# Start of a two-branch token mixer: copies behind their own transposes, 1/std spread ahead of the third group, C of block 1 held, one more warm-up matmul

## Chip, cores, metric

One core of one Trainium2 chip. The metric is the device time of one execution in microseconds (us). The profile's span is about 1.75 us shorter than the time of the same execution; differences of spans and of times can be compared with each other. Batches of runs were on different chips, so each run is compared with runs of the kernel before that were made beside it on its own chip, unless something else is said.

## The reference, cut to what matters

```python
xn = layernorm(x)                       # x: 2048 tokens x 576, bf16
# branch A: a diagonal complex state space model, 576 states, scanned over the tokens
h[t] = Lam_bar * h[t-1] + B_bar @ xn[t]
y[t] = 2 * Re(C @ h[t]) + xn[t] * Dskip
# branch B: a gated unit, 576 -> 4608 -> 576
b = (sigmoid(xn @ w_gate) * (xn @ w_up)) @ w_down
out = x + y + b
```

The kernel works on four blocks of 512 tokens. The gated unit's products (gate/up groups and `w_down` pairs) fill TensorE. The scan runs on VectorE beside them, and "C of block nb" is the product of C with the states of one block, added to the output of that block.

## The kernel before: the parts concerned

The first ten groups of block 0 are "raw": they multiply centred but not yet scaled x, and the scale 1/std per token is put in when a group is emptied from PSUM. PSUM is four buffers of two banks (`ps`), and they are handed from user to user. The start:

```python
start_groups = [RawGateUp(0, f, 0) for f in range(2)]
ptrs = [psum.tile([P, 2, TB], FP32, name="ptr", tag="ps") for _ in range(2)]
def ptr(tt):                                   # tiles 0, 1 in buffer 0; tiles 2, 3 in buffer 1
    return ptrs[tt // 2][:, tt % 2, 0:6 * H].bitcast(BF16).rearrange(...)
...
busy(7, TB)                                    # warm-up: 7 matmuls of 512 columns on zeros
start_mean(0, nc.vector); start_mean(1, nc.scalar)
xc0 = start_centre(0, nc.vector); xc1 = start_centre(1, nc.scalar)
start_transpose(2, xts[2]); start_transpose(0, xc0)
start_transpose(1, xc1);    start_transpose(3, xts[3])
for tt in range(2):
    nc.vector.tensor_copy(xc_part(tt), ptr(tt)[:, 0:RC + 1, :])
start_mean(2, nc.scalar); start_mean(3, nc.scalar)
over_rows(pmean(2), negm[:, 2:3])              # spread a column over rows: an fp32 transpose
busy(4, P)
start_centre_rows(2)
for g in start_groups: g.turn(0, first)        # tokens 0 to 255
over_rows(pmean(3), negm[:, 3:4]); start_centre_rows(3)
for g in start_groups: g.turn(1, first)
... # squares, 1/std on ScalarE and VectorE, statistics of block 1 on VectorE
... # second halves of both groups (tokens 256 to 511)
third = RawGateUp(0, 2, 0); third.open(); third.turn(0)
consts_transpose(ptr(3)[:, RC, :])
for tt in range(TT_B):
    over_rows(ptrs[1][:, 0, tt * P:(tt + 1) * P], rstds[0][:, tt:tt + 1])
consts_copy(ptr(3)[:, RC, :])                  # three small copies on VectorE
nc.scalar.copy(scale0[:], ptrs[1][:, 0, :])    # the fourth group takes this buffer
```

And C of block 1, which is issued as soon as the last state operation of the block is queued:

```python
def between_steps():
    if 1 in ssm_done and 1 not in c_done and glu_done[0]:
        for tl in range(0, TT_B, 2):
            d_pair([TT_B + tl, TT_B + tl + 1], [c_terms(1, tl), c_terms(1, tl + 1)], True, True)
        c_done.add(1)
```

Of the kernel before, what the change touches and what calls it, by code (L numbers as in the profile page):

```python
# [12 lines left out]
FP32 = mybir.dt.float32  # L13
BF16 = mybir.dt.bfloat16
# [52 lines left out]
def kernel(  # L67
# [17 lines left out]
    nc = tc.nc  # L85
    P = 128
    H = 64
# [7 lines left out]
    TB = 512  # L95
# [3 lines left out]
    TT_B = TB // P  # L99
    KF = D // P  # L100
    R0 = KF * P
    PT = NS // P
    NU = PT + 1
# [3 lines left out]
    NH = D // H  # L107
    FP = 2
    RC = R0 // P
# [12 lines left out]
    hpool = ctx.enter_context(tc.tile_pool(name="hpool", bufs=1))  # L122
# [84 lines left out]
    cvals = consts.tile([P, 3, NU], FP32, name="cvals")  # L207
    ldt, lre, lim = (cvals[:, i, :] for i in range(3))
    def consts_transpose(ps):
        for half in (slice(0, H), slice(H, P)):  # L210
            nc.tensor.transpose(ps[half, 0:3 * NH], crows[:], ident[0:3 * NH, 0:3 * NH])

    def consts_copy(ps):

        rows = ps[:, 0:3 * NH].rearrange("p (i a) -> p i a", a=NH)
        nc.vector.tensor_copy(cvals[0:H, :, :], rows[0:H, :, 0:NH:2])
        nc.vector.tensor_copy(cvals[H:P, :, 0:PT], rows[H:P, :, 1:NH:2])
        nc.vector.tensor_copy(cvals[H:P, :, PT:NU], rows[H:P, :, NH - 1:NH])

    iota = ssmp.tile([P, TB], FP32, name="iota", tag="buim", bufs=2)  # L220
    nc.gpsimd.iota(iota[:], pattern=[[1, TB]], base=0, channel_multiplier=0,
# [8 lines left out]
    rstds = {}  # L230
# [5 lines left out]
    def ln_stats(tt):  # L236
        nb, tl = divmod(tt, TT_B)
        if tl == 0:
            mvs[nb] = lnp.tile([P, TT_B, nc.vector.BN_AGGR_DIM], FP32, name="mv")
            rstds[nb] = lnp.tile([P, TT_B], FP32, name="rstd")  # L240
        xt = xts[tt]
        st = lnp.tile([P, 2, BN], FP32, name="bnst")
        for gi in range(2):
            nc.vector.bn_stats(st[:, gi, :], xt[:, gi * DH:(gi + 1) * DH])
        nc.vector.bn_aggr(mvs[nb][:, tl, :], st[:])
# [8 lines left out]
    negm = consts.tile([P, TT_B], FP32, name="negm")  # L254
    ssq = consts.tile([P, TT_B], FP32, name="ssq")

    def start_mean(tt, eng):
        junk, m = xn_bufs[tt % 2], negm[:, tt:tt + 1]
        if eng is nc.vector:
            nc.vector.tensor_scalar(junk[:, 0:D], xts[tt][:], -1.0 / D, None, ALU.mult, ALU.add, accum_out=m)  # L260
        else:
            nc.scalar.activation(junk[:, 0:D], xts[tt][:], ACT.Copy, scale=-1.0 / D, accum_out=m)
# [188 lines left out]
    hst = {}  # L451
# [7 lines left out]
    def ssm_w(nb, pt, part):  # L459
        bre, bim = bu[(nb, pt)]  # L460
        t1, t2 = T1[:, pt, :], T2[:, pt, :]
        if part == 0:
            tmps["w"] = ssmp.tile([P, 2, TB], BF16, name="wrim", tag="wrim")
        w = tmps["w"][:, part, :]
        a, b = (bre, bim) if part == 0 else (bim, bre)
        tq = bft("tq", 2)
        nc.vector.tensor_mul(w, t1, a[:])
        nc.vector.tensor_mul(tq[:], t2, b[:])
        if part == 0 and pt < PT:
            nc.vector.tensor_sub(w, w, tq[:])  # L470
        else:
            nc.vector.tensor_add(w, w, tq[:])
# [32 lines left out]
    def ssm_h(nb, pt, part):  # L505
        gre, gim = tmps["gre"], tmps["gim"]
        c, s = C2[:, pt, :], S2[:, pt, :]
        tq = bft("tq", 2)
        if part == 0:
            h = hpool.tile([P, 2, TB], BF16, name="hst", tag="hst", bufs=10)  # L510
            hst[(nb, pt)] = h
            nc.vector.tensor_mul(h[:, 0, :], c, gre[:])
            nc.vector.tensor_mul(tq[:], s, gim[:])  # L513
            nc.vector.tensor_add(h[:, 0, :], h[:, 0, :], tq[:])  # L514
        else:
            h = hst[(nb, pt)]
            nc.vector.tensor_mul(h[:, 1, :], s, gre[:])
            nc.vector.tensor_mul(tq[:], c, gim[:])
            nc.vector.tensor_sub(h[:, 1, :], h[:, 1, :], tq[:])


    bg = Background()
# [130 lines left out]
    def c_terms(nb, tl):  # L653
        ts_ = slice(tl * P, (tl + 1) * P)
        terms = []
        for pt in range(PT):
            terms.append((hst[(nb, pt)][:, 0, ts_], ctre[:, pt, :]))
            terms.append((hst[(nb, pt)][:, 1, ts_], ctim[:, pt, :]))
        terms.append((hst[(nb, PT)][:, 0, ts_], ctp[:]))
        return terms  # L660
# [105 lines left out]
    glu_done = [False]  # L766
    ln_done = set()
    ssm_done = set()
    c_done = set()
    bu_wanted = deque()  # L770
    chain = [(nb, pt) for nb in range(NB) for pt in range(NU)]

    def want_bu(i):
        if i < len(chain):
            bu_wanted.append(chain[i])

    def queue_ssm(i):
        nb, pt = chain[i]

        def bu_ready():  # L780
            return (nb, pt) in bu and bu_at[(nb, pt)] + 2 <= bg.now

        def h_ready():
            return nb < 2 or (nb - 2) in c_done

        bg.add(1.85, lambda: ssm_w(nb, pt, 0), ready=bu_ready)
        if pt < PT:
            bg.add(1.85, lambda: ssm_w(nb, pt, 1))
        else:
            bg.add(0.0, lambda: None)  # L790
        bg.add(0.0, lambda: want_bu(i + 2))
        bg.add(1.3, lambda: ssm_scan(nb, pt, 0))
        bg.add(2.0 if pt < PT else 1.2, lambda: ssm_scan(nb, pt, 1))
        bg.add(1.3, lambda: ssm_h(nb, pt, 0), ready=h_ready)
        if pt < PT:
            bg.add(1.3, lambda: ssm_h(nb, pt, 1))
        if pt == NU - 1:
            bg.add(0.0, lambda: ssm_done.add(nb))


    n_slots = NSB * NC
# [36 lines left out]

    def between_steps():

        if 1 in ssm_done and 1 not in c_done and glu_done[0]:
            for tl in range(0, TT_B, 2):
                d_pair([TT_B + tl, TT_B + tl + 1], [c_terms(1, tl), c_terms(1, tl + 1)], True, True)
            c_done.add(1)
# [26 lines left out]
    start_groups = [RawGateUp(0, f, 0) for f in range(2)]  # L871
    ptrs = [psum.tile([P, 2, TB], FP32, name="ptr", tag="ps") for _ in range(2)]

    def ptr(tt):
        return ptrs[tt // 2][:, tt % 2, 0:6 * H].bitcast(BF16).rearrange("p (c t) -> p c t", t=P)

    def pmean(tt):
        return ptrs[tt // 2][:, tt % 2, 6 * H:8 * H]

    for g in start_groups:  # L880
        g.open()
# [1 line left out]
    def busy(n, cols):  # L883
        for i in range(n):
            zeros = warm[:].unsqueeze(1).to_broadcast([P, cols // P, P])
            nc.tensor.matmul(start_groups[0].ps[:, i % 2, 0:cols], warm[:], zeros, start=True, stop=True)

    def start_transpose(tt, src):
        for c in range(RC):
            nc.tensor.transpose(ptr(tt)[:, c, :], src[:, c * P:(c + 1) * P], ident[:])  # L890
        for rows in (LO, HI):
            nc.tensor.transpose(ptr(tt)[rows, RC, :], src[:, R0:D], ident[:])

    def over_rows(dst, col):
        nc.tensor.transpose(dst, col.to_broadcast([P, P]), ident32[:])  # L895

    def xc_part(tt):
        return xcT[:, :, tt * P:(tt + 1) * P]

    def start_centre(tt, eng):  # L900
        xc = xn_bufs[2 + tt]
        if eng is nc.vector:
            nc.vector.tensor_scalar_add(xc[:, 0:D], xts[tt][:], negm[:, tt:tt + 1])
        else:
            nc.scalar.activation(xc[:, 0:D], xts[tt][:], ACT.Identity, bias=negm[:, tt:tt + 1])
        return xc
# [5 lines left out]
        nc.vector.tensor_add(xc_part(tt), ptr(tt)[:, 0:RC + 1, :],  # L912
                             mrow[:, tt % 2, :].unsqueeze(1).to_broadcast([P, RC + 1, P]))

    busy(7, TB)
    start_mean(0, nc.vector)
    start_mean(1, nc.scalar)
    xc0 = start_centre(0, nc.vector)
    xc1 = start_centre(1, nc.scalar)
    start_transpose(2, xts[2])  # L920
    start_transpose(0, xc0)
    start_transpose(1, xc1)
    start_transpose(3, xts[3])
    for tt in range(2):
        nc.vector.tensor_copy(xc_part(tt), ptr(tt)[:, 0:RC + 1, :])
    start_mean(2, nc.scalar)
    start_mean(3, nc.scalar)
    over_rows(pmean(2), negm[:, 2:3])
    busy(4, P)
    start_centre_rows(2)  # L930
    first = slice(0, 2 * P)
    for g in start_groups:
# [6 lines left out]
        start_square(tt)  # L939
    rstds[0] = lnp.tile([P, TT_B], FP32, name="rstd")  # L940
    nc.scalar.activation(rstds[0][:], ssq[:], ACT.Sqrt, bias=eps_t[:], scale=1.0 / D)
    for tt in range(TT_B, TT_B + 2):
        ln_stats(tt)
    ln_recip(0, 0, TT_B)
    for tt in range(TT_B + 2, 2 * TT_B):
        ln_stats(tt)
    for t in range(2):
        for g in start_groups:
            if t == 0:
                g.hold()  # L950
            g.turn(t, slice(2 * P, TB))
    third = RawGateUp(0, 2, 0)
    third.open()
    third.turn(0)
    consts_transpose(ptr(3)[:, RC, :])
    for tt in range(TT_B):
        over_rows(ptrs[1][:, 0, tt * P:(tt + 1) * P], rstds[0][:, tt:tt + 1])
    consts_copy(ptr(3)[:, RC, :])
    scale0 = hpool.tile([P, TB], FP32, name="scale0", tag="hst", bufs=10)
    nc.scalar.copy(scale0[:], ptrs[1][:, 0, :])  # L960
    ln_std(1, 0, TT_B)
    exp_first()
    for g in start_groups:
# [9 lines left out]
    for f in range(3, NRAW + 1):  # L973
        tt = order0.popleft()
# [19 lines left out]
    for sb in range(NSB):  # L994
        b0 = sb * NB_SB
        for c in range(NC):
# [30 lines left out]
            for tt in range(0, NB_SB * TT_B, 2):  # L1027
                nbl, tl = divmod(tt, TT_B)
                nb = b0 + nbl
# [48 lines left out]
```

## Time and profile before

| | kernel before |
|---|---|
| median of the first three runs, us (range) | 509.88 (508.89 to 510.25) |
| time and span of the profiled execution, us | 508.75, 507.0 |
| TensorE busy, us | 499.4 |
| first products of the second halves, us | 10.50 |
| fourth raw group starts, us | 15.62 |
| C of block 1, us | 254.31 to 265.35 |

TensorE is busy for nearly the whole span, so only its own waits are worth anything. The lines of the waits, of the chain and of the timeline that carry this stand in the prediction below. Columns of the chain are start, duration, and what ran; in the timeline a bracket at the end of a line gives the idle time before it and what ended it. "PE L890" is TensorE at line 890.

### The profile page before, as it was taken

To read this page: it belongs to the slowest core of one execution; us is meant where nothing else is said; L and a number is where in the kernel's file an instruction comes from. 1 tells how busy PE (TensorE), PEld (TensorE's weight loads), DVE (VectorE), ACT (ScalarE), POOL (GpSimd) and SP (SyncE) were. 2 spreads that over 40 slices of the span, in tenths; PEclk is the share of its full clock that TensorE was granted. 3 is DMA by queue.
4 is the path that set the end of the run, shared out by engine and by line. 5 is a ranking of instruction groups with operands and counts; after the bars stand their busy time and mean duration, and the time that the engine had idled before them with its cause. 6 is when DMAs were issued, how large, how long until landed. Compare 5 with 4: busy or idle time off the path is not lost.

```text
span 507.0 us, 13273 instructions
## 1 busy us (share of the span) xinstructions
PE 499.4 (99%) x5827; PEld 311.3 (61%) x5827; DVE 325.1 (64%) x697; ACT 214.5 (42%) x391; POOL 104.8 (21%) x148
## 2 busy tenths in 40 slices
PE   8999999999999999999999999999999999999997
PEld 5455796555697555699764445764445774446774
DVE  5879799787694777868777666947666842221121
ACT  6875593555400755610124564015565005553000
POOL 9677100133110043110001331000431101300000
PEclk9999999999999999999999999999999999999999
DMA  8548531244343094221301541100632100500001
GB/s 241 131 82 247 160 77 48 67 120 131 78 114 89 15 239 121 65 73 45 70 25 37 174 131 43 43 26 1 185 94 76 47 27 15 187 0 3 25 26 47
DMA packets 36495, 43.36 MB, mean 86 GB/s; under 512 B 25238, under 2 KB 28886, under 8 KB 36438
## 3 DMA queue, kind: packets, MB, share of 16 engines
q0 software_dynamic: 9520, 32.60, 21.7%
q1 hardware_dynamic: 26486, 9.60, 8.7%
q8 instruction: 45, 0.74, 0.6%
q10 hardware_dynamic: 432, 0.33, 0.3%
q14 instruction: 12, 0.10, 0.1%
HBM read 34.36 MB, written 2.36 MB: 72 GB/s over the span
## 4 chain that ended last, share of the span: by engine, by line
PE 97%; DMA 1%; DVE 1%; issue 0%; ACT 0%; POOL 0%; POOLq 0%; ACTq 0%
PE pgu L532 55%; PE pd L709 33%; PE pbu L532 7%; PE pd L669 1%; DMA wgu<-in_B_w_up_dram 1%; PE pd L677 1%; POOL wgu L157 0%; PE ptr L895 0%; DVE xT L912 0%; ACT sT L570 0%; ACT scale L960 0%; ACT uT L571 0%; DVE hst L514 0%; DVE hT L573 0%; DVE tq L513 0%
## 5 line engine op out<-in xcount | busy, mean ns | idle before, releaser
L532 PE MATMUL pgu<-xT,wgu 64*128 64x512 bf16 (+1 forms) x2336 | 278.1, 373 | 1.6 <-ACT scale L960 1.2
L532 PEld LDWEIGHTS <-wgu 64*128 64x128 bf16 x2336 | 123.3, 94 | 123.9 <-issue 1.8
L570 ACT ACTIVATE sT<-pgu 128x512 bf16<-128x512 f32 x134 | 80.1, 598 | 150.9 <-PE pgu L532 150.9
L709 PE MATMUL pd<-wd,hT 64*128 64x288 bf16 x2208 | 140.2, 283 | 0.0
L573 DVE TENSOR_TENSOR hT<-sT,uT 128x512 bf16<-128x512 bf16 x134 | 56.8, 424 | 119.8 <-ACT uT L571 119.5
L709 PEld LDWEIGHTS <-hT 64*128 64x128 bf16 x2208 | 117.0, 94 | 20.5
L571 ACT CAST uT<-pgu 128x512 bf16<-128x512 f32 x134 | 77.7, 580 | 0.0
L157 POOL DMA_DIRECT2D wgu<-in_B_w_gate_dram x36 | 28.0, 777 | 225.9 <-PE pgu L532 225.8
L532 PE MATMUL pgu<-xT,wrem 64*128 64x512 bf16 (+1 forms) x292 | 56.5, 373 | 0.0
L171 POOL DMA_DIRECT2D wd<-in_B_w_down_dram x36 | 25.6, 712 | 96.9 <-PE pd L709 71.5
L620 ACT COPY bure<-pbu 128x512 f32<-128x512 f32 x16 | 9.4, 587 | 82.6 <-PE pbu L532 81.7
L727 DVE TENSOR_TENSOR acc<-acc,pd 128x576 f32<-128x576 f32 x36 | 25.4, 747 | 13.6 <-PE pd L709 13.6
L532 PE MATMUL pbu<-xT,bt 64*128 64x512 bf16 x256 | 32.1, 376 | 0.0
L709 PEld LDWEIGHTS <-hst 64*128 64x128 bf16 x504 | 25.8, 94 | 6.8 <-issue 0.8
L709 PE MATMUL pd<-ctre,hst 64*128 64x288 bf16 x224 | 29.0, 283 | 0.5 <-ACT uT L571 0.5
L709 PE MATMUL pd<-ctim,hst 64*128 64x288 bf16 x224 | 28.8, 283 | 0.0
L157 POOL DMA_DIRECT2D wgu<-in_B_w_up_dram x36 | 27.1, 753 | 0.0
L481 DVE TENSOR_TENSOR_SCAN gre<-r,g0re,wrim 128x512 bf16<-128x512 f32 x20 | 25.6, 1279 | 0.1
L532 PEld LDWEIGHTS <-wrem 64*128 64x128 bf16 x292 | 15.6, 94 | 15.8
L724 DVE TENSOR_TENSOR ob<-acc,pd 128x576 bf16<-128x576 f32 x14 | 9.9, 748 | 23.3 <-PE pd L709 23.3
L532 PEld LDWEIGHTS <-bt 64*128 64x128 bf16 x256 | 13.8, 94 | 13.1
L488 DVE TENSOR_TENSOR_SCAN gim<-r,g0im,wrim 128x512 bf16<-128x512 f32 x16 | 20.3, 1266 | 0.0
(159 smaller groups left out, 365.3 us busy)
## 6 DMA issues: line engine op xcount, KB each, us to landing
wd<-in_B_w_down_dram POOLq DMA_DIRECT2D x36, 288.0 KB, 4.4
wgu<-in_B_w_gate_dram POOLq DMA_DIRECT2D x36, 256.0 KB, 3.5
wgu<-in_B_w_up_dram POOLq DMA_DIRECT2D x36, 256.0 KB, 3.8
out_dram<-ob SPq DMA_DIRECT2D x15, 144.0 KB, 1.8
xt<-in_A_x_dram SPq DMA_DIRECT2D x10, 144.0 KB, 3.2
wrem<-in_B_w_gate_dram POOLq DMA_DIRECT2D x5, 192.0 KB, 5.1
wrem<-in_B_w_up_dram POOLq DMA_DIRECT2D x5, 192.0 KB, 5.1
xt<-in_A_x_dram POOLq DMA_DIRECT2D x4, 144.0 KB, 3.9
```

The lines of the kernel that those rows point to most:

```text
L157: nc.gpsimd.dma_start(w[:, gi, :, :], src[0:R0, fs].rearrange("(c p) f -> p c f", p=P))
L171: nc.gpsimd.dma_start(wd[:], B_w_down[f0:f0 + FP * P, :].rearrange("(n p) d -> p n d", p=P))
L481: nc.vector.tensor_tensor_scan(gre[:], r_bc, w[:, 0, :], g0re[:, col], ALU.mult, ALU.add)
L488: nc.vector.tensor_tensor_scan(gim[:], r_bc, w[:, 1, :], g0im[:, col], ALU.mult, ALU.add)
L532: m = nc.tensor.matmul(self.ps[:, which, cols], lhsT, rhs, start=start, stop=stop)
L570: nc.scalar.activation(sT[:], self.ps[:, 0, :], ACT.Sigmoid)
L571: nc.scalar.copy(uT[:], self.ps[:, 1, :])
L573: nc.vector.tensor_mul(h[:], sT[:], uT[:])
L620: nc.scalar.copy(bre[:], self.ps[:, 0, :])
L709: m = nc.tensor.matmul(pds[k][:, a, 0:DH], lhsT[rows, :], rhs[rows, a * DH:(a + 1) * DH], start=turn == 0 and i == 0, stop=turn == 1 and i ...
L724: nc.vector.tensor_add(halves(ob[:]), halves(acc[:]), pd[:, :, 0:DH])
L727: nc.vector.tensor_add(halves(acc[:]), halves(acc[:]), pd[:, :, 0:DH])
```

## The change

The intent: to let the copies of token tiles 0 and 1 start behind their own transposes, to have 1/std spread and copied while the third group's products run, so that the fourth group finds its buffer free, and to keep C of block 1 from being issued before its inputs are there. The three small copies of constants go from VectorE to ScalarE, and the warm-up in front is eight matmuls in place of seven, with the four small ones before the first products dropped.

```diff
--- before.py
+++ after.py
@@ -213,9 +213,9 @@
     def consts_copy(ps):
 
         rows = ps[:, 0:3 * NH].rearrange("p (i a) -> p i a", a=NH)
-        nc.vector.tensor_copy(cvals[0:H, :, :], rows[0:H, :, 0:NH:2])
-        nc.vector.tensor_copy(cvals[H:P, :, 0:PT], rows[H:P, :, 1:NH:2])
-        nc.vector.tensor_copy(cvals[H:P, :, PT:NU], rows[H:P, :, NH - 1:NH])
+        nc.scalar.copy(cvals[0:H, :, :], rows[0:H, :, 0:NH:2])
+        nc.scalar.copy(cvals[H:P, :, 0:PT], rows[H:P, :, 1:NH:2])
+        nc.scalar.copy(cvals[H:P, :, PT:NU], rows[H:P, :, NH - 1:NH])
 
     iota = ssmp.tile([P, TB], FP32, name="iota", tag="buim", bufs=2)
     nc.gpsimd.iota(iota[:], pattern=[[1, TB]], base=0, channel_multiplier=0,
@@ -766,6 +766,7 @@
     glu_done = [False]
     ln_done = set()
     ssm_done = set()
+    ssm_at = []
     c_done = set()
     bu_wanted = deque()
     chain = [(nb, pt) for nb in range(NB) for pt in range(NU)]
@@ -796,6 +797,7 @@
             bg.add(1.3, lambda: ssm_h(nb, pt, 1))
         if pt == NU - 1:
             bg.add(0.0, lambda: ssm_done.add(nb))
+            bg.add(0.0, lambda: ssm_at.append(bg.now) if nb == 1 else None)
 
 
     n_slots = NSB * NC
@@ -838,7 +840,7 @@
 
     def between_steps():
 
-        if 1 in ssm_done and 1 not in c_done and glu_done[0]:
+        if ssm_at and ssm_at[0] + 3 <= bg.now and 1 not in c_done and glu_done[0]:
             for tl in range(0, TT_B, 2):
                 d_pair([TT_B + tl, TT_B + tl + 1], [c_terms(1, tl), c_terms(1, tl + 1)], True, True)
             c_done.add(1)
@@ -871,11 +873,14 @@
     start_groups = [RawGateUp(0, f, 0) for f in range(2)]
     ptrs = [psum.tile([P, 2, TB], FP32, name="ptr", tag="ps") for _ in range(2)]
 
+    PLACE = {0: (0, 0), 3: (0, 1), 2: (1, 0), 1: (1, 1)}
+
     def ptr(tt):
-        return ptrs[tt // 2][:, tt % 2, 0:6 * H].bitcast(BF16).rearrange("p (c t) -> p c t", t=P)
+        i, j = PLACE[tt]
+        return ptrs[i][:, j, 0:6 * H].bitcast(BF16).rearrange("p (c t) -> p c t", t=P)
 
     def pmean(tt):
-        return ptrs[tt // 2][:, tt % 2, 6 * H:8 * H]
+        return ptrs[0][:, tt % 2, 6 * H:8 * H]
 
     for g in start_groups:
         g.open()
@@ -912,21 +917,23 @@
         nc.vector.tensor_add(xc_part(tt), ptr(tt)[:, 0:RC + 1, :],
                              mrow[:, tt % 2, :].unsqueeze(1).to_broadcast([P, RC + 1, P]))
 
-    busy(7, TB)
+    def start_copy(tt):
+        nc.vector.tensor_copy(xc_part(tt), ptr(tt)[:, 0:RC + 1, :])
+
+    busy(8, TB)
     start_mean(0, nc.vector)
     start_mean(1, nc.scalar)
     xc0 = start_centre(0, nc.vector)
     xc1 = start_centre(1, nc.scalar)
+    start_mean(2, nc.scalar)
+    start_mean(3, nc.scalar)
     start_transpose(2, xts[2])
     start_transpose(0, xc0)
+    start_copy(0)
     start_transpose(1, xc1)
+    start_copy(1)
+    over_rows(pmean(2), negm[:, 2:3])
     start_transpose(3, xts[3])
-    for tt in range(2):
-        nc.vector.tensor_copy(xc_part(tt), ptr(tt)[:, 0:RC + 1, :])
-    start_mean(2, nc.scalar)
-    start_mean(3, nc.scalar)
-    over_rows(pmean(2), negm[:, 2:3])
-    busy(4, P)
     start_centre_rows(2)
     first = slice(0, 2 * P)
     for g in start_groups:
@@ -939,25 +946,24 @@
         start_square(tt)
     rstds[0] = lnp.tile([P, TT_B], FP32, name="rstd")
     nc.scalar.activation(rstds[0][:], ssq[:], ACT.Sqrt, bias=eps_t[:], scale=1.0 / D)
-    for tt in range(TT_B, TT_B + 2):
-        ln_stats(tt)
+    ln_stats(TT_B)
     ln_recip(0, 0, TT_B)
-    for tt in range(TT_B + 2, 2 * TT_B):
+    for tt in range(TT_B + 1, 2 * TT_B):
         ln_stats(tt)
     for t in range(2):
         for g in start_groups:
             if t == 0:
                 g.hold()
             g.turn(t, slice(2 * P, TB))
+    consts_transpose(ptr(1)[:, RC, :])
+    for tt in range(TT_B):
+        over_rows(ptrs[1][:, 0, tt * P:(tt + 1) * P], rstds[0][:, tt:tt + 1])
+    scale0 = hpool.tile([P, TB], FP32, name="scale0", tag="hst", bufs=10)
+    nc.scalar.copy(scale0[:], ptrs[1][:, 0, :])
+    consts_copy(ptr(1)[:, RC, :])
     third = RawGateUp(0, 2, 0)
     third.open()
     third.turn(0)
-    consts_transpose(ptr(3)[:, RC, :])
-    for tt in range(TT_B):
-        over_rows(ptrs[1][:, 0, tt * P:(tt + 1) * P], rstds[0][:, tt:tt + 1])
-    consts_copy(ptr(3)[:, RC, :])
-    scale0 = hpool.tile([P, TB], FP32, name="scale0", tag="hst", bufs=10)
-    nc.scalar.copy(scale0[:], ptrs[1][:, 0, :])
     ln_std(1, 0, TT_B)
     exp_first()
     for g in start_groups:
```

## The prediction

> **What bounds the kernel now.** I read, in this order: the page's busy shares, the waits of TensorE by themselves, the chain that ended last in order of time, and the timeline around each wait that this left. The busy shares and the waits of TensorE come first, because they say how much there is to win at all.
>
> ```profile
> PE 499.4 (99%) x5827; PEld 311.3 (61%) x5827; DVE 325.1 (64%) x697; ACT 214.5 (42%) x391; POOL 104.8 (21%) x148
> ...
> PE pgu L532 <- ACT scale L960: 1.2, 1, 1.2
> PE pgu L886 <- DVE zero_t L200: 1.0, 1, 1.0
> PE ptr L890 <- DMA xt<-in_A_x_dram: 0.5, 1, 0.5
> PE pd L709 <- DVE hst L514: 0.5, 1, 0.5
> PE pd L709 <- ACT uT L571: 0.5, 1, 0.5
> PE pgu L532 <- DVE xT L912: 0.3, 1, 0.3
> ```
>
> TensorE is busy for 499.4 of 507.0 us, and all its listed waits add up to 4.0 us. The change removes no products, so it can win only from this list. The second and third waits (launch, and the first load of x) lie before anything that the diff moves. That leaves the first, the fourth and the fifth, and perhaps the last. The chain shows where the first comes from (columns: start, duration, what):
>
> ```profile
> 2.33 5.25 DMA wgu<-in_B_w_up_dram
> ...
> 7.62 1.38 PE pgu L532 x19
> ...
> 9.62 0.83 DVE xT L912
> ...
> 10.50 3.22 PE pgu L532 x46
> ...
> 13.85 0.60 PE ptr L895 x4
> ...
> 14.47 0.17 DVE cvals L216
> ...
> 14.82 0.09 DVE cvals L218
> ...
> 14.99 0.59 ACT scale L960
> 15.58 0.04 issue
> 15.62 40.97 PE pgu L532 x378
> ```
>
> Two things are to be seen. First, up to 7.6 us the start hangs on the load of the first up weights, not on the transposes. Second, after the spread of 1/std (four fp32 transposes, L895) TensorE does nothing from 14.43 to 15.62: VectorE makes its three small copies of constants, only then ScalarE copies the scale, and only then the fourth gate/up group gets the PSUM buffer that both copies read. From there the chain stays on TensorE until about 252 us. The timeline there:
>
> ```profile
> 252.62 1.28 ACT L570 ACT_TABLE_LOAD   x1 [0.91 <-PE pgu L532]
> ...
> 254.31 0.28 PE L709 MATMUL pd<-ctre,hst 64*128 64x288 bf16 x1
> ...
> 255.04 0.28 PE L709 MATMUL pd<-ctre,hst 64*128 64x288 bf16 x1 [0.45 <-ACT uT L571]
> ...
> 256.63 0.30 PE L709 MATMUL pd<-ctp,hst 64*128 64x288 bf16 x2 [0.46 <-DVE hst L514]
> ...
> 265.35 1.03 PE L532 MATMUL pbu<-xT,bt 64*128 64x512 bf16 x8
> ```
>
> This is C of block 1, the two pairs of products that turn the states of token block 1 into output. It is issued the moment its last state is queued on VectorE. Its second PSUM buffer is not free yet, because ScalarE had to load a table before it could empty it (wait 0.45), and its last state is not written yet (wait 0.46).
>
> [...]with two row halves side by side: 18 matmuls of 512 columns take 1.94 us in the chain, nine times 216 ns; and the stretch from 214.38 to 247.58 us holds 264 pairs of 288 columns and 4 pairs of 512, which is 32.34 + 0.86 = 33.20 us, exactly the stretch. I use these two as the rate without waits. [...]The trace has 1.28 us for each load and 586 ns for the 512-column scale copy[...]. [...]In the trace the keeping apart goes by the whole buffer of two banks: the scale copy (bank 0) started at 14.99 us, after the constants' copies (bank 1) ended at 14.90; and the copy of token tile 0 at 6.27 us began after the transposes of tile 1 (end 6.23), although those of tile 0 ended at 5.73. That is why the change moves tiles to other buffers. [...]The trace's first transposes at 4.62 us already take 219 ns[...], after seven warm-up matmuls from 1.00 us.
>
> **The change part by part.**
>
> Warm-up: one more matmul of 512 columns at the front and four of 128 fewer before the first products. The seven ran from 1.00 to 4.17 us, spaced about 0.43. The eighth ends near 4.6, inside the 0.46 us wait for x. The four small ones (6.83 to 7.22) stand before a wait for weights that ends at 7.62. Cost and gain 0.
>
> Copies and places: tile 0's copy (0.49 us) can start at about 5.77 in place of 6.27, and tile 1's at 6.27 in place of 6.75, so both are done near 6.75 rather than 7.16. The spread of tile 2's mean now waits for tile 0's copy (about 6.25), and the transposes of tile 3 end near 7.0. All is ready by 7.0 to 7.1, but the first real products wait for the up weights until 7.62, and within the first half turns for the remainder weights until about 8.17. After that, the mean of tile 3, its 0.82 us add and the restart at 10.50 keep their order and their lengths. Gain 0; what comes is slack of 0.4 us.
>
> 1/std earlier: VectorE inverts after the statistics of one tile rather than two. The one costs about 1.0 us (10.36 to 11.41), so the result stands at about 11.5 instead of 12.37. ScalarE's square root is done at 9.94. The half turns of the first two groups end at 12.46 (36 matmuls of 256 columns, 18 x 0.109 = 1.96 us from 10.50), so the spread will not wait.
>
> Spread ahead of the third group: before, the third group's last products hold the array until 13.54, and the fourth starts at 15.62. That is 2.08 us for constants' transposes, spread and copies. The transposes and spread alone take from 13.54 to about 14.3 (last start 14.16 plus its columns), 0.75 us, and stay. After the change they stand at 12.46 to 13.25, and their results are in at about 13.35. The third group's 10 matmuls (5 x 0.216 = 1.08) then run to about 14.33. Beside them ScalarE makes the scale copy (13.40 to 13.99) and then the three small ones, which are now on ScalarE[...]. The buffer is free at about 14.35. So the fourth group starts at 14.35 to 14.5, not at 15.62. The gain is 1.1 to 1.25 us; I take 1.2.
>
> Is it kept? The followers move too. VectorE ends its statistics at 14.25 and starts the first scaled evacuation then (15.60 before). ScalarE's table load follows the square root for block 1 at about 14.7 (15.79 before), so its row of sigmoids and norms starts about 1.1 us earlier. The two places with least room later: the last transposed tile of block 1 lands at about 28.4 us for a use at 29.2 (room 0.8), and the ninth raw group's buffer is empty at 34.4 for a use at 35.0 (room 0.6). Both suffice for a difference of 0.1.
>
> C of block 1 held by three steps: the work is the same, only later, with about 6 us of groups in between. Its own length without waits is 72 pairs x 0.1225 + 4 x 0.216 = 9.68 us; it took 265.35 - 254.31 = 11.04. The loss is thus 1.36 us, more than the 0.91 in the list of waits, because the ends of matmuls are modelled and the first wait also split a pair. After the hold the last state (written at 256.59) and the evacuation (254.99) are done long before. What takes its place are groups whose buffers are free at 251.7 and 254.99, needed at 254.3 and about 256.3. Nobody else needs the result soon: the states of block 3, and accumulators first used at 312 us. Gain 1.36.
>
> Sum: 1.2 + 0 + 1.36 = 2.55 us. 509.88 - 2.55 = 507.3; I say 507.4, because a little of it may be lost in new small waits.
>
> **The rivals.** (1) The small copies become the new wait: if each takes 0.3 us on ScalarE without overlap, the buffer is free at about 14.9, and the start wins only 0.7. [...]for it, that ScalarE's small operations with a bias operand here took 300 ns (L248). Time 507.9. (2) The start's gain is given back at 29 or 35 us, because ScalarE's row does not move as far as TensorE. It was busy without a pause from 14.99 to 25.66. The rooms of 0.8 and 0.6 speak against it. Time 508.0 to 508.5. (3) The gain of copies and places is real, the start moving earlier as a whole by 0.3 to 0.4. The chain's DMA until 7.58 speaks against it. Time 507.0. (4) Held C meets another wait, a buffer just being emptied or VectorE's row displaced. At the other changes from groups to pairs (56, 135, 312 us) the trace has no wait. Time 508.7.[...]
>
> **Range and chances.** The runs before spread from 508.89 to 510.25, so a median of three moves by some 0.5 us on its own. Both gains full give 507.3; one lost gives 508.5 or 508.7; a small extra gives 506.8. The range for 8 in 10 is 506.5 to 508.6. Two per cent is 10 us, more than all waits together, and a slower kernel by as much would need a new wait repeated many times: faster by over 2% 0.005, within 2% 0.99, slower 0.005.
>
> **What would show it.** Right: the chain after the spread goes from TensorE to TensorE, the wait for the scale shrinks from 1.2 to at most 0.2 us, and the fourth group starts near 14.4; the first products still wait for the up weights until about 7.6; both waits of L709 are gone, and C's stretch takes 9.7 us. Wrong: a wait of the fourth group for a copy of constants over 0.4 us, a new TensorE wait near 28, 34 or 260 us, or first products well before 7.6. Unequal landing of the first weights in the two profiles would disturb the comparison of the start; I would then compare from 10.5 us on.

## The result, and the profile after

The changed kernel took 505.98 us (median of 4 runs, 505.87 to 506.29) beside 509.38 (median of 4, 508.34 to 510.25): a ratio of 0.9935, with a 95% interval of 0.9914 to 0.9957. The time lies below the range of the prediction (506.5 to 508.6).

TensorE's waits in the profile after, all that the view lists:

```profile
PE pgu L891 <- DVE zero_t L200: 1.0, 1, 1.0
PE pgu L532 <- DVE xT L917: 0.3, 1, 0.3
```

The waits for the scale, for the last state and for the evacuation are gone, and the wait for the first x too, since the longer warm-up covers it (it runs to 4.59 us, and the transposes start at 4.54). The chain of the profile after, from the first products on:

```profile
7.55 1.20 PE pgu L532 x20
...
9.37 0.83 DVE xT L917
...
10.25 2.14 PE pgu L532 x36
...
12.52 0.58 PE ptr L900 x4
13.10 42.02 PE pgu L532 x388
```

The chain now goes from the spread (L900) straight back to products. In the timeline the fourth group's first products are at 14.12 us, behind ten of the third group. The start of the second halves moved by 0.25 us (10.50 to 10.25), and the way from there to the fourth group shrank from 5.12 to 3.87 us, by 1.25. C of block 1 in the timeline after:

```profile
254.68 0.43 DVE L514 TENSOR_TENSOR hst<-hst,tq 128x512 bf16<-128x512 bf16 x1
...
258.66 0.30 PE L709 MATMUL pd<-ctre,hst 64*128 64x288 bf16 x2
...
268.34 1.04 PE L532 MATMUL pgu<-xT,wgu 64*128 64x512 bf16 x8
```

The last state is written 3.5 us before C starts, and C takes 268.34 - 258.66 = 9.68 us, the length without waits. The three differences (0.25, 1.25 and 1.36) make up the difference of the two spans, 507.0 - 504.2 = 2.8 us, to within 0.06. So the two profiles differ by little more than the predicted 2.55. The timed runs differ by more, 3.4 us by the medians. Where the rest comes from is the question of most experiments below.

### The profile page after: what moved, and what is told of

Its sections match the earlier page's. It is cut to its first block, busy times and chain, and to the rows that moved or that the text cites. A ratio compares the mean times of both kernels' runs of the same rounds, so it can differ in the third digit from the quotient of the medians. Undisturbed runs are those within 1.5% of the kernel's fastest.

```text
span 504.2 us, 13269 instructions
## 1 busy us (share of the span) xinstructions
PE 499.3 (99%) x5824; PEld 333.8 (66%) x5824; DVE 324.8 (64%) x694; ACT 215.0 (43%) x394; POOL 104.7 (21%) x148
## 4 chain that ended last, share of the span: by engine, by line
PE 99%; DVE 0%; issue 0%
PE pgu L532 55%; PE pd L709 33%; PE pbu L532 7%; PE pd L669 1%; PE pd L677 1%; PE pgu L891 1%; PE ptr L895 0%; PE ptr L900 0%; PE ptr L897 0%; DVE xT L917 0%; DVE mrow L916 0%; DVE ob L678 0%; PE ptr L211 0%; DVE warm L194 0%; DVE zero_t L200 0%
## 5 line engine op out<-in xcount | busy, mean ns | idle before, releaser
L532 PEld LDWEIGHTS <-wgu 64*128 64x128 bf16 x2336 | 131.5, 94 | 114.0 <-issue 0.8
L709 PE MATMUL pd<-wd,hT 64*128 64x288 bf16 x2208 | 140.5, 283 | 0.0
L709 PEld LDWEIGHTS <-hT 64*128 64x128 bf16 x2208 | 125.9, 94 | 11.6
L709 PEld LDWEIGHTS <-hst 64*128 64x128 bf16 x504 | 28.7, 94 | 2.5
L709 PE MATMUL pd<-ctim,hst 64*128 64x288 bf16 x224 | 29.1, 283 | 0.0
L709 PE MATMUL pd<-ctre,hst 64*128 64x288 bf16 x224 | 29.1, 283 | 0.0
```

Of the source, the lines that this page charges most:

```text
L532: m = nc.tensor.matmul(self.ps[:, which, cols], lhsT, rhs, start=start, stop=stop)
L709: m = nc.tensor.matmul(pds[k][:, a, 0:DH], lhsT[rows, :], rhs[rows, a * DH:(a + 1) * DH], start=turn == 0 and i == 0, stop=turn == 1 and i ...
```

## The experiments

All outputs are right. "Long" and "short" are explained with the first one. A saving "against the short class" is taken from the mean of that class over all chips; taken from the short executions on the run's own chip it differs by at most 0.12 us.

### The kernel before, against itself

No edit.

> The unchanged kernel against itself. The two profiles differ by 2.8 us of span, the timed medians by 3.4 us; the four runs of the kernel before spread over 1.9 us, those of the changed kernel over 0.4. Theory A (the start of the old kernel varies from execution to execution, by the landing of the first loads or the moment at which the array clock goes to full speed, and its profile happened to be one of the short ones): ratio 1.000, runs again spread over 1 to 2 us, and if this profile's span is over 507.5, the excess lies before 15.6 us. Theory B (the four runs of before were merely a bad draw): the spread is under 0.6 us and the median near 508.7.

Measured: ratio 0.9993 (0.997 to 1.0015). Its six times are 508.40, 508.43, 508.51 and 509.86, 510.21, 510.23; the eleven of the kernel before beside it split in the same way. Over this whole study the kernel before ran 55 times: 34 **short** executions (508.04 to 508.89, mean 508.46) and 21 **long** ones (509.83 to 511.13, mean 510.25), with nothing between. The profiled execution is a long one this time, span 508.4. The two profiles side by side, first that of the prediction (short), TensorE's timeline:

```profile
4.62 0.40 PE L890 MATMUL ptr<-ident,xt 128*128 128x128 bf16 x4 [0.46 <-DMA xt<-in_A_x_dram]
...
6.16 0.40 PE L890 MATMUL ptr<-ident,xt 128*128 128x128 bf16 x4
...
7.21 1.01 PE L532 MATMUL pgu<-xT,wgu 64*128 64x256 bf16 x8
...
10.50 0.61 PE L532 MATMUL pgu<-xT,wgu 64*128 64x256 bf16 x8 [0.26 <-DVE xT L912]
```

and the long one:

```profile
4.46 0.61 PE L890 MATMUL ptr<-ident,xt 128*128 128x128 bf16 x4 [0.30 <-DMA xt<-in_A_x_dram]
...
6.83 0.61 PE L890 MATMUL ptr<-ident,xt 128*128 128x128 bf16 x4
...
8.45 1.04 PE L532 MATMUL pgu<-xT,wgu 64*128 64x256 bf16 x8
...
11.96 0.61 PE L532 MATMUL pgu<-xT,wgu 64*128 64x256 bf16 x8 [0.26 <-DVE xT L912]
```

x arrives even earlier in the long one, but four transposes take 0.61 us in place of 0.40, to the last: the array still runs at a lower rate ("cold"). Its first eight products fill 0.82 us (8.45 to 9.27), eight equal ones at the start of the second halves 0.43 (11.96 to 12.39), so the lower rate is about half. The first products come at 8.45 us with their weights already there, and the second halves start 1.46 us later. After that the two executions are alike (from the second halves to the fourth group 5.12 us in both). So the excess lies before 10.5 us, and it is the array's rate, not a load. The profile page's row of the granted clock does not show it; in the long execution's windows (after the range: length, busy time and count of PE, PEld, DVE, ACT and POOL, then the granted clock, the share and the rate of DMA) it reads 1.00 while the array is cold:

```profile
5.50:6.50 1.00, 1.00 (x10) 0.56 (x7) 0.00 (x0) 1.00 (x5) 1.00 (x3) 1.00 0.95 201
```

What follows: theory A holds, in its form with the array's speed. The profile that the prediction was worked out from is of the short class; the median that it started from, 509.88, is a long execution.

### C held, old start

```diff
-        if 1 in ssm_done and 1 not in c_done and glu_done[0]:
+        if ssm_at and ssm_at[0] + 3 <= bg.now and 1 not in c_done and glu_done[0]:
```

(with `ssm_at` set as in the change). 

> The old start, with only C of block 1 held. Both theories: 1.34 to 1.36 us less than before (ratio 0.9973), both waits of L709 gone, the start as in before with its wait for the scale of 1.2 us. Theory A: the spread of the times stays as wide as that of before (1 to 2 us). If instead the waits at C were what varies, the spread falls to about 0.4 us.

Measured: median 507.29 (506.72 to 507.74, six runs), mean 507.24, against the short class's 508.46: 1.2 us less. The ratio of 0.9956 (0.9938 to 0.9974) holds more than that, since six of the eleven executions beside it were long. Both waits of L709 are gone, the wait for the scale (1.2) is there. None of the six was long, although the start is that of before. Theory A had expected a spread as wide as before (1 to 2 us); the 1.0 measured just meets that, but the long executions that make the spread of before are not in it. It was run again below.

### New start, C not held

The change without the edit above.

> The new start, C of block 1 not held. Theory A: 1.5 us less than before by the profiles, up to 2.1 by the timed runs, and the spread is narrow (0.4 us), since what varied was in the old start. Theory B: 1.2 to 1.5 us less in both. The two waits of L709 are there, about 0.9 us together.

Measured: 507.03 (506.86 to 507.46), mean 507.09, ratio 0.9954 (0.9936 to 0.9971): 1.37 us less than the short class, 1.16 more than the changed kernel. The waits of L709 are there (0.5 and 0.4). The times are narrow (0.6 us), as theory A expects; the ratio is a larger step than it named, since six of the eleven executions beside it were long.

### The changed kernel again

> The changed kernel once more. Theory A: 2.8 to 3.4 us less than before, the sum of the two parts, spread about 0.4 us. Theory B: 2.6 to 2.8 us less. The profile shows whether the first products start at 7.5 us again and whether the load of the up weights or of the remainder weights is waited for this time.

Measured: 505.88 (505.59 to 506.10), ratio 0.9929 (0.9912 to 0.9947): by the means 3.7 us less than the eleven executions beside it, more than either theory named, again since six of these were long. In its profile four transposes fall from 0.63 to 0.40 us at 5.19 us and the up weights are waited for until 7.55 (0.21 us); in the first profile they fall only at 6.99 us, and nothing is waited for. The second halves start at 10.47 and 10.25 us. Over four profiles with the new start (two of the changed kernel, C not held, and the hold of one step below) they start at 9.93 to 10.47 us, over the three short profiles of the kernel before at 9.97 to 10.50. So the 0.25 us by which the first pair of profiles differed there is not a gain of the change: it comes and goes with the landing of the first weights and the moment of the full rate. The ten executions of the changed kernel (505.59 to 506.29) have a mean of 505.93, and none is long.

### One more warm-up matmul, nothing else

```diff
-    busy(7, TB)
+    busy(8, TB)
```

> The kernel before with one more warm-up matmul of 512 columns and nothing else. The profile of the long execution of before (508.4 us) had the array at half rate until about 9 us, in the short one (507.0) it was at full rate at 4.6 us. Clock theory: [...]with the gap filled the long class (510.0 to 511.0) disappears, the short class (508.1 to 508.9) stays where it is, the mean falls by 0.7 to 0.9 us (ratio 0.9985). Rival (the first loads vary): both classes remain and the ratio is 1.000.

Measured: all six executions short, 508.19 to 508.56, ratio 0.998 (0.9961 to 0.9998); five of the eleven beside it were long. The short class stays where it is. If 5 of 11 is the rate, six short ones in a row have a chance of 3%. This run has a gap of 0.29 us ahead of the transposes too, since its x came late (4.88 us), and four transposes still fell to 0.40 us by 5.50. A gap by itself does not decide, then; that no execution is long is as the clock theory expected. Over the whole study, none of 39 executions of kernels with eight warm-up matmuls was long.

### The changed kernel with the old warm-up

```diff
-    busy(8, TB)
+    busy(7, TB)
...
     start_transpose(3, xts[3])
+    busy(4, P)
     start_centre_rows(2)
```

> The changed kernel with the old warm-up: seven matmuls of 512 columns in front, four of 128 before the first products. Clock theory: two classes appear, one near 505.9 and one 1 to 1.5 us above it, mean some 0.7 us over the changed kernel. Rival (another part of the new start narrowed the times): 505.6 to 506.3 as before.

Measured: 505.97 (505.80 to 506.18), all six like the changed kernel. The expectation of the clock theory was wrong here: seven matmuls did not bring two classes back. In its profile the transposes followed the warm-up without a pause (4.23 us).

### The order alone

On top of eight warm-up matmuls: 1/std inverted after one tile's statistics, the spread ahead of the third group. Constants and places as before.

```diff
+    consts_transpose(ptr(3)[:, RC, :])
+    ... # spread, consts_copy on VectorE, scale copy
     third = RawGateUp(0, 2, 0)
     third.open()
     third.turn(0)
-    consts_transpose(ptr(3)[:, RC, :])
-    ... # spread, consts_copy on VectorE, scale copy
```

> The kernel before, with eight warm-up matmuls as in the run beside it, and of the change only the order: 1/std inverted after one tile's statistics and its spread ahead of the third group. Constants still on VectorE ahead of the scale copy, old buffers. Against the eight-warm-up kernel: the chain spread, three copies (0.44), scale copy (0.59), 1.19 in all, now lies beside 1.08 us of the third group: a wait of 0.1 to 0.2 us is left, gain 1.0 to 1.1 us. If the copies' place on VectorE were what cost, the gain would be under 0.5 us.

Measured: 508.18 (508.01 to 508.42) beside 508.36 of the eight-warm-up kernel: 0.18 us. By the profiles, from the second halves to the fourth group it takes 4.78 us in place of 5.13: a gain of 0.35, not of 1.0 to 1.1, and a wait of 0.7 us is left. The chain of this run says why:

```profile
13.86 0.21 DVE mv L245
14.07 0.03 DVE cvals L216
...
14.45 0.59 ACT scale L956
15.05 0.04 issue
15.09 40.97 PE pgu L532 x378
```

The spread was done at 13.1 us, but the copies of the constants are queued behind VectorE's statistics of block 1, which end at 14.07 us here and between 14.08 and 14.25 in the profiles of the kernel before, with seven and with eight warm-up matmuls. In the old order these statistics ended just before the spread did, so they never showed. The low alternative of the expectation was the right one.

### The constants' copies on ScalarE alone

On top of eight warm-up matmuls, the third group still ahead of the spread:

```diff
-    consts_copy(ptr(3)[:, RC, :])            # on VectorE
     scale0 = hpool.tile([P, TB], FP32, name="scale0", tag="hst", bufs=10)
     nc.scalar.copy(scale0[:], ptrs[1][:, 0, :])
+    consts_copy(ptr(3)[:, RC, :])            # on ScalarE
```

> The kernel before, with eight warm-up matmuls, and of the change only the three constants' copies on ScalarE behind the scale copy; the third group still ahead of the spread. The profile of the changed kernel has the three copies end 0.89 us after the scale copy starts, against 1.19 us from the end of the spread to the fourth group before: the wait of the fourth group falls from 1.2 to 0.9 or 1.0 us, gain 0.2 to 0.3 us.

Measured: 508.21 (508.00 to 508.55), by the means 0.08 us less than the eight-warm-up kernel; by the profiles 4.90 us in place of 5.13, a gain of 0.23, as expected. The timed runs of this one and the one before it show less than the profiles, but they also contain the start, which moves by some 0.5 us between executions; the stretches of the profiles do not. Its chain:

```profile
14.46 0.59 ACT scale L959
...
15.28 0.07 ACT cvals L218
15.35 0.04 issue
15.39 40.97 PE pgu L532 x378
```

Apart, the two parts win 0.35 and 0.23; together, in the changed kernel, 1.25. The rest is their interaction: behind the statistics in VectorE's queue the copies cannot make use of the earlier spread, on ScalarE they can. Putting them ahead of the statistics on VectorE, which might do the same, was not tried.

### Five warm-up matmuls

```diff
-    busy(7, TB)
+    busy(5, TB)
```

> The kernel before with five warm-up matmuls in place of seven: a warm-up of about 2.2 us and then a gap of 0.9 to 1.3 us until the first x is there. Of 32 executions of the kernel before so far 16 were long (509.8 to 511.1), of 48 of the other eight kernels none, though two of them had the same seven warm-up matmuls; their profiles showed gaps under 0.1 us, those of before 0.3 and 0.46. Clock theory[...]: nearly all executions are now long, 510 to 511 us, and the profile has transposes of 0.61 us for four until the first products. Rival (the long class is a matter of the load of x or of the image of the program, not of the clock's warm-up): the two classes as in before, about half and half, or only the short one.

(The text counts 48 executions of eight kernels; it was 46 executions in eight runs of seven kernels.) Measured: all five executions in the long class, 509.72 to 510.66, ratio 1.0027 (1.001 to 1.0043); of the nine beside them two were long. TensorE's timeline of this run:

```profile
4.26 0.61 PE L890 MATMUL ptr<-ident,xt 128*128 128x128 bf16 x4 [0.95 <-DMA xt<-in_A_x_dram]
...
8.24 1.04 PE L532 MATMUL pgu<-xT,wgu 64*128 64x256 bf16 x8
```

This makes the long class at will, at an x that lands early. That a cold array is what it is made of counts as shown. (That it is the array's clock is not shown: the granted clock reads 1.00 in the cold windows of the first experiment's long execution. What the traces show is that equal operations take longer, 0.61 against 0.40 us for four transposes, and that the length of the warm-up alone brings this about.)

### The changed kernel with five warm-up matmuls

The same edit (eight to five) in the changed kernel.

> The changed kernel with five warm-up matmuls in place of eight. Clock theory: it falls into a long class too, 1.0 to 1.6 us over 505.9, so that the new places and copies do not protect against a cold array. Rival (the new places are what narrowed the times): 505.6 to 506.5 as before.

Measured: 507.11 (506.45 to 507.41), mean 507.00, 1.07 us over the changed kernel's 505.93. The new places do not protect against a cold array, though the loss is smaller than before's (510.30 - 508.46 = 1.84).

### C held, old start, once more

> Old start, C held, once more. Its first six executions were all short (506.7 to 507.7) although its start is that of before. If those were luck, two classes appear: 506.9 and 508.6. If again none is long, the classes of before do not come from the instructions of the start alone, and what decides stays open.

Measured: 507.03 (506.88 to 507.15), ratio 0.9963 (0.995 to 0.9977); none of five long. With the first run, none of eleven. Two of the nine executions of the kernel before beside it were long. So the warm-up's length and the instructions of the start are not all that decides.

### A hold of one step

```diff
-        if ssm_at and ssm_at[0] + 3 <= bg.now and ...
+        if ssm_at and ssm_at[0] + 1 <= bg.now and ...
```

> The changed kernel with a hold of one step in place of three. By the waits, C would start 1.9 us later than without a hold; the evacuation it waited for (0.73 us of start to start) and the last state (0.73 us) are then ready, so 505.9 us as with three steps. If the table load's delay or VectorE's row reaches further, a wait at the first pair remains and the time is 0.2 to 0.7 us over it.

Measured: 506.89 (506.81 to 507.00), as with no hold at all (507.09). The expectation took a step for one group, which it is not. Both waits are back in the profile:

```profile
PE pd L709 <- DVE hst L514: 0.5, 1, 0.5
PE pd L709 <- ACT uT L571: 0.5, 1, 0.5
```

and C starts behind the same products as without a hold (8 of the second state input), so the count has moved on by at least one before the test is made and a hold of one is none. How long a hold the two waits need was not tested; three is enough.

### C held, six warm-up matmuls

```diff
-    busy(7, TB)
+    busy(6, TB)
```

in the held kernel with the old start.

> The kernel with C held and the old start, but six warm-up matmuls in place of seven, so that a gap of about 0.5 us opens between warm-up and transposes (its profiles with seven showed under 0.1 us; those of before, with the same seven, 0.3 and 0.46). If the gap is what makes the long class, it appears here: some or all executions near 508.5, the others at 506.9 to 507.7. If none is long, a gap of half a microsecond is not enough and the class of before comes from something else.

Measured: 506.56 to 507.07 four times, 508.24 and 509.53: long executions appear in this kernel too. Only the longest one was profiled: a gap of 0.94 us, transposes of 0.61 us to the last, products at 8.66. So with six matmuls the kernel with C held is not immune. With seven, none of its eleven executions was long; why, this run does not tell.

### Three more looks at the kernel before

> The unchanged kernel, one profile. Clock theory: if the time is over 509.7, four transposes take 0.61 us up to the last of them and the first products start after 8 us; if it is under 509, they fall to 0.40 us before 6.7 us. In both, the loads of x and of the up weights land within 0.5 us of each other. Rival: a long run with transposes of 0.40 us and a late load.

> As the look before: a long run has transposes of 0.61 us throughout, a short one has them fall to 0.40 us before 6.7 us; the rival expects a late load in the long run.

> As the two looks before: the same two outcomes by class. Over the five profiles of this kernel, the gap ahead of the first transposes tells whether a gap of 0.3 us and more occurs only in the long class (two profiles so far, one of each class, both with a gap).

Measured: 508.26, 508.31 and 510.02. The first look, TensorE's timeline:

```profile
4.11 0.61 PE L890 MATMUL ptr<-ident,xt 128*128 128x128 bf16 x4
...
5.14 0.40 PE L890 MATMUL ptr<-ident,xn 128*128 128x128 bf16 x4 [0.17 <-DVE xn L903]
```

and the third:

```profile
4.36 0.61 PE L890 MATMUL ptr<-ident,xt 128*128 128x128 bf16 x4 [0.20 <-DMA xt<-in_A_x_dram]
...
6.72 0.61 PE L890 MATMUL ptr<-ident,xt 128*128 128x128 bf16 x4
```

As expected of each class; in none of the three did TensorE wait for the up weights ahead of the first products, so no late load stands behind the long one. Over the five profiles of this kernel: without a gap (4.11 and 4.18 us) two short; with gaps of 0.20 and 0.30 us two long; with a gap of 0.46 us one short, which was at full rate when its transposes began. So every long execution that was profiled has a gap behind the warm-up, but a gap does not make every execution long.

**What stays open.** Why the kernel before falls into the long class in 21 of 55 executions, while the two other kernels with seven warm-up matmuls (C held, and the changed kernel with the old warm-up) did so in none of 17. In the three profiles of those, x was there within some 0.13 us of the end of the warm-up; in three of the five of the kernel before it came later. Whether that is a property of the program, or of the executions that happened to be profiled, no run here tells. A late x is not peculiar to the kernel before: over all 18 profiles the first weight load with x starts between 4.11 and 4.88 us, at 4.35 or later in three of its five and in three of the 13 others. And a second thing varies from execution to execution: without any gap, and with eight warm-up matmuls both times, the full rate came before 4.4 us (hold of one step) or only at about 6.65 us (changed kernel, first profile). That the two together decide is a guess. Nor was it tested whether transposes, which are all that the array does from the end of the warm-up to the first products but for the four small matmuls, bring the full rate about as the warm-up's matmuls do.

## Why the prediction was wrong

**The start level: wrong.** The failed step is the last line of the sum, "509.88 - 2.55 = 507.3", together with the sentence on the range, that "a median of three moves by some 0.5 us on its own". The 2.55 was worked out from an execution of the short class (508.75 us, and the difference to the median was there to be seen), and was subtracted from a median that was an execution of the long class (509.88). The spread of 1.4 us over three runs was taken for noise around one level; it was two levels 1.8 us apart. From the mean of the short class the sum gives 508.46 - 2.55 = 505.91; the changed kernel's ten executions have a mean of 505.93. (The terms add up to 2.56; the text has 2.55.) That it comes so close is partly luck, since the runs scatter by more than 0.02. In part the miss was bad luck too: at the rate of 21 in 55, a median of three is a long execution in about one case of three.

**Warm-up: right about the wait, but the long class was left out.** The step said "Cost and gain 0", since the eighth matmul fits into a wait. It does. But with the change the long class is gone, which is worth 21/55 x 1.78 = 0.68 us on average. Of the whole difference of means, 509.14 - 505.93 = 3.21 us, this is what the prediction lacked. None of its rivals has two classes of executions; the runs show that pauses of 0.2 to 0.3 us stand behind the warm-up in the long executions of the kernel before. The one matmul alone left all six executions short, and five in place of eight cost the changed kernel 1.07 us. That a warm-up cut to five makes the long class is shown; that the eighth matmul is what takes it away is not. With eight and the old start none of 18 executions was long, but neither was any of 17 with seven in the two other kernels, so which part of the change removes it stays open.

**Copies and places: right in the sum, not tested alone.** On the chip where both ran, the changed kernel is 1.38 us below the kernel with C held and the old start (505.86 and 507.24, means), of which the spread is 1.25; that leaves about 0.1 for copies, places and warm-up, so of rival (3), 0.3 to 0.4 us, little is seen. But one of the prediction's signs of being wrong did come: first products well before 7.6 us, at 6.86 (C not held) and 6.75 us (hold of one step). There the weights are then waited for within the first turns, as at 7.55 us in the second profile of the changed kernel, and the second halves start within the same half microsecond in both kernels' short executions. So the wait "until 7.62" belongs to one execution; the loads land at different times.

**Spread ahead of the third group: right**, 1.25 us for a predicted 1.1 to 1.25, and with no wait left. The fourth group started at 14.12, and at 14.35 in the second profile, against a predicted 14.35 to 14.5. That the three copies on ScalarE would leave the buffer free at about 14.35 was the estimate; no trace before the change showed it. They ended 0.89 us after the scale copy's start (13.14 to 14.03). But the prediction did not say how much hung on the copies' move to ScalarE; the expectation of the order alone shows that I thought it a detail. Without it the order wins 0.35 of the 1.25 us. Rival (1) did not happen: the copies took 0.16 to 0.17 us.

**Kept later: right.** There is no new wait of TensorE anywhere. Rivals (2) and (4) did not happen.

**C held: right**, 1.36 us predicted, 1.36 in C's own stretch, 1.2 to 1.4 in the timed runs. (Its length without waits rests on the rates of the trace before: 1.94 us for nine pairs of 512 columns, 0.216 us a pair, and 32.34 us for 264 pairs of 288 columns, 0.1225 us a pair. The 0.109 us of a pair of 256 columns, used for the half turns, is close to the 1.08 us that ten pairs took from 10.50 us on.)

## What to carry to other kernels

Before a sum is taken off a time, see whether that time and the profile are of the same class: list the single runs, and if they fall into two groups, profile both before explaining either. The list of waits was too small here, where two row halves run side by side: the length of a stretch against its length at the rate without waits gave 1.36 us where the list gave 0.91, and the timed runs (1.2 to 1.4) bear out the longer figure. And a copy that is moved forward in one engine's order gains only if its own engine's queue lets it: here the same reordering was worth 0.35 us with the small copies on VectorE behind its statistics, and 1.25 with them on ScalarE.

## What the traces showed beside the change

- With seven or eight warm-up matmuls from 1.0 us on, the cold rate ended anywhere from before 4.4 to about 6.65 us, and later than 9 us in the long executions. After 3.17 us of warm-up, executions with pauses of 0.20 and 0.30 us right behind it stayed cold past the transposes, one with 0.46 us did not.
- The longer stretch at the cold rate costs the long class 1.8 us of 510, 0.35%, and that is more than the whole gain of either part of the change (1.25 and 1.36).
- The granted clock of the profile read 1.00 while the array ran at its cold rate; the length of four equal transposes (0.61 against 0.40 us) was the sign to go by.
- The program's waits kept ScalarE and VectorE apart by the buffer of two banks (scale copy at 14.99 us behind copies of the other bank that ended at 14.90). In the kernel before, the fourth group had to wait for the one after the other (0.44 and 0.59 us).
- The three small copies, which the trace names CAST, took 158 to 165 ns each on ScalarE, and 159 to 175 on VectorE before.
